# SiLU written with tanh, and half of the attention rows divided on ScalarE: an attention block with two feed-forward layers on one core

## The chip, the core and the metric

The kernel runs on one core of one Trainium2 chip. A core has TensorE (PE, with the weight loads PEld beside the matmuls), VectorE (DVE), ScalarE (ACT), GpSimd (POOL), and SyncE (SP), which issues the transfers. The metric is the device time of one execution in microseconds; lower is better.

## The reference, cut to what matters

Attention over 4 batches of 8 heads, 512 local and 32 global positions of 64 values, is followed by two feed-forward layers on 2176 tokens of 512 values. The first layer, which the change touches, is a gated SiLU with 1536 inner features; the second has 2048 inner features and a leaky ReLU with a slope per feature.

```python
def sm(s):
    s = s - np.max(s, axis=-1, keepdims=True)
    e = np.exp(s)
    return e / (np.sum(e, axis=-1, keepdims=True) + 1e-09)
...
def _moe_ref(x, w_gate, w_val, w_out):
    g = x @ w_gate
    silu = g * (1.0 / (1.0 + np.exp(-g)))
    val = x @ w_val
    return (silu * val @ w_out).astype(np.float32)
```

## The kernel before

The feed-forward products are made as three matmul passes over pairs of tiles: every operand is split into an upper part in a short format and the remainder, so each block of 128 features needs 12 matmuls (`mm12`, line 519). Weights arrive in a packed form and are converted on chip: two ScalarE passes (lines 454 and 455), three VectorE passes (456, 457, 460), a copy for the upper part (472 on ScalarE or 470 on VectorE) and a subtraction for the remainder (435, VectorE).

**Attention units.** A local unit is one pair of heads and one half (256 rows) of the positions; a batch has eight local units and two global ones. `s` makes the scores (line 171), takes the row maxima on VectorE (184) and the exponentials with their row sums on ScalarE (197). `n` makes the reciprocals of the sums (204, 205) and divides the four 128x256 pieces of the unit (207, VectorE). `t` transposes the result, for batches 0 and 1 on TensorE (229) with a ScalarE copy out of PSUM (154), and for batches 2 and 3 (`split`) by a DMA after a rounding to half precision (221, 222). `pv` makes the product with the values (250 or 241) and writes it into the token tile: for batch 0 straight into the operand `xa` of the first layer (264, 265), for the others to `yp` or `y3` (258).

**Stages.** The first units of batch 0 run ahead of everything else. Then `visit1` runs the first layer for one batch (or a part of its columns) and one half of the inner features (`GA` or `GB`), and `pump` puts the steps of the attention units between its pieces, so that batch 1 to 3 attention runs beside the first layer of batches 0 to 2. Each step of a unit is put into the queue in the order `s`, `t` of the unit before, `n`, `pv` of the one before that. The first layer of batch 3 has no attention beside it. The second layer (`visit2`) comes last.

**Inside visit1.** For a group of up to 512 columns: 12 or 24 matmuls into the PSUM bank `g`; `Silu` on ScalarE from that bank to the SBUF tile `sg` (576); the same number of matmuls into the bank `v`; their product on VectorE to `t` (585); the upper part `h` on ScalarE (589) and the remainder on VectorE (593, queued at the next `pump`). The matmuls of `down` (559) of a group run one or two groups later. There is one bank `g`, one bank `v`, one `sg` and one `t`. Work goes to the engines in order of priority and readiness as the framework plans it; each engine then runs its queue in that fixed order.

In the profile a load of ScalarE's function table (ACT_TABLE_LOAD) stands before the first exponential after a SiLU and before the first SiLU after an exponential. The copies and the Relus have none.

Of the kernel before, what the change touches and what calls it, by code (L numbers as in the profile page):

```python
# [17 lines left out]
ACTF = mybir.ActivationFunctionType  # L18
ALU = mybir.AluOpType
# [23 lines left out]
def kernel(  # L43
# [11 lines left out]
    nc = tc.nc  # L55
    HEAT, ND, NR, LAG = (P[i] for i in ("HEAT", "ND", "NR", "LAG"))

    def pr(name):
        off = P["pr_" + name]
        return tc.high_priority(off) if off else nullcontext()  # L60
# [3 lines left out]
    def frac(name):  # L64
        a = mix.get(name, 0.0) + P[name]
        mix[name] = a - int(a + 1e-9)
        return int(a + 1e-9) > 0
# [30 lines left out]
    def bank(tag):  # L98
        return ps.tile([128, 512], F32, tag=tag, name="ps_" + tag)
# [11 lines left out]
    def heat(n):  # L111
        t = bank("g")
        for _ in range(n):
            nc.tensor.matmul(out=t[:, 0:128], lhsT=zero, rhs=zero, start=True, stop=True)
# [44 lines left out]
    class Local(Unit):  # L159
# [42 lines left out]
        def n(self):  # L202
            rc = attp.tile([128, 4], F32, tag="rc", name="rc")
            nc.vector.tensor_scalar(out=rc, in0=self.sm, scalar1=1e-9, scalar2=None, op0=ALU.add)
            nc.vector.reciprocal(out=rc, in_=rc)
            for j in range(4):
                nc.vector.tensor_scalar(
                    out=self.e[:, j], in0=self.e[:, j], scalar1=rc[:, j:j + 1],
                    scalar2=PSC if self.split else None, op0=ALU.mult,
                    op1=ALU.mult if self.split else ALU.bypass,  # L210
                )
            if self.split and self.half == 0:
                self.pair.split_v()
# [137 lines left out]
    def later(n, f):  # L351
        due.setdefault(st["k"] + n, []).append(f)
# [141 lines left out]
    def weight(key):  # L494
        while key not in wt:
            if not wloaded and not wsplit and not wlo:
                wload()
            wpump()
        return wt[key]
# [6 lines left out]
    def passes(a, b):  # L506
        return ((a[0], b[0]), (a[0], b[1]), (a[1], b[0]))
# [5 lines left out]
    def mm12(o, w, c0, c1):  # L513
        i = 0
        for k in range(4):
            wk = [w[:, p, 128 * k:128 * k + 128] for p in range(2)]
            xk = [xa[:, p, k, c0:c1] for p in range(2)]
            for a, x in passes(wk, xk):
                nc.tensor.matmul(out=o, lhsT=a, rhs=x, start=(i == 0), stop=(i == 11))  # L519
                i += 1  # L520

    def ypieces(b, c0, c1):
        res = []
        for hf in range(2):
            a, z = max(c0, 256 * hf), min(c1, 256 * hf + 256)
            if a < z:
                res.append((lambda m, hf=hf, a=a, z=z: yh(b, hf)[:, m, a - 256 * hf:z - 256 * hf], a - c0, z - a))
        if c1 > S:
            res.append((lambda m: yg[:, m], S - c0, 128))
        return res  # L530
# [4 lines left out]
    def visit1(b, c0, c1, fs, last, pump, after_f=None, boundary=None, third=None):  # L535
        n = c1 - c0
        half = n == 256
        acc = [bank(f"acc{m}") for m in range(2 if half else 4)]
        if half:
            acc = [acc[m // 2][:, 256 * (m % 2):256 * (m % 2) + 256] for m in range(4)]  # L540
        hs = {}

        per = max(1, 512 // n)
        groups = [fs[i:i + per] for i in range(0, len(fs), per)]
        nn = n * per
        lag = 2 if third else 1

        def down(i):
            h = hs.pop(i)
            for q, f in enumerate(groups[i]):  # L550
                w = weight((1, f, "o"))
                opens = None
                for m in range(4):
                    wm = [w[:, p, 128 * m:128 * m + 128] for p in range(2)]
                    second = half and m % 2 == 1
                    for j, (a, x) in enumerate(passes(wm, [h[:, p, n * q:n * q + n] for p in range(2)])):
                        first = f == fs[0] and j == 0
                        with tc.issue_after(opens.ins) if first and second else nullcontext():
                            mm = nc.tensor.matmul(  # L559
                                out=acc[m][:, 0:n], lhsT=a, rhs=x,  # L560
                                start=(first and not second),
                                stop=(f == fs[-1] and j == 2 and (second or not half)),
                            )
                        if first:
                            opens = mm
                if after_f:
                    after_f(f, "o")

        for i, gf in enumerate(groups):
            pump()  # L570
            g = bank("g")
            for q, f in enumerate(gf):
                mm12(g[:, n * q:n * q + n], weight((1, f, "g")), c0, c1)
            sg = work.tile([128, 512], F32, tag="sg", name="sg")
            with pr("h"):
                nc.scalar.activation(out=sg[:, 0:nn], in_=g[:, 0:nn], func=ACTF.Silu)  # L576
            pump()
            v = bank("v")
            for q, f in enumerate(gf):
                mm12(v[:, n * q:n * q + n], weight((1, f, "v")), c0, c1)  # L580
                if after_f:
                    after_f(f, "gv")
            t = work.tile([128, 512], F32, tag="t", name="t")
            with pr("h"):
                nc.vector.tensor_tensor(out=t[:, 0:nn], in0=v[:, 0:nn], in1=sg[:, 0:nn], op=ALU.mult)  # L585
            h = third() if third and i % 3 == 2 else hp.tile([128, 2, 512], F32R, tag="h", name="h")
            hs[i] = h
            with pr("h"):
                nc.scalar.activation(out=h[:, 0, 0:nn], in_=t[:, 0:nn], func=ACTF.Copy)
            zh = "0" if st["k"] < mark[1] else "1" if st["k"] < mark[2] else "2" if st["k"] < mark[4] else "3"  # L590
            eng = nc.gpsimd if frac("hq" + zh) else nc.vector
            soon.append(
                lambda h=h, t=t, eng=eng: eng.tensor_tensor(
                    out=h[:, 1, 0:nn], in0=t[:, 0:nn], in1=h[:, 0, 0:nn], op=ALU.subtract
                )
            )
            pump()
            if i >= lag:
                down(i - lag)
        if boundary:  # L600
            boundary()
        for i in range(max(0, len(groups) - lag), len(groups)):
            down(i)
        with pr("acc"):
            for m in range(4):
                if (c0, c1) == (0, S):
                    dst = yp[b][:, :, m]
                    src = acc[m].rearrange("p (a c) -> p a c", a=2)
                    if last:
                        nc.vector.tensor_tensor(out=dst, in0=src, in1=dst, op=ALU.add)  # L610
                    else:
                        nc.scalar.activation(out=dst, in_=src, func=ACTF.Copy)
                    continue
                for dst, o, z in ypieces(b, c0, c1):
                    if last:
                        nc.vector.tensor_tensor(out=dst(m), in0=acc[m][:, o:o + z], in1=dst(m), op=ALU.add)
                    else:
                        nc.scalar.activation(out=dst(m), in_=acc[m][:, o:o + z], func=ACTF.Copy)
# [74 lines left out]
    if True:  # L693
# [47 lines left out]
        def reload(group, first):  # L741
# [9 lines left out]
            return after  # L751

        visit1(0, 0, 256, GA, False, pumper(P["ns0"], mark[1] + P["e0"], P["wr0"], P["g0"]), third=early)
        p = pumper(P["ns1"], mark[2] + P["e1"], P["wr1"], P["g1"])
        assert st["k"] >= mark[1] + LAG
        visit1(0, 256, 512, GA, False, p, after_f=reload(GB, GA), third=early)
        att_tags["list"] = ["a0", "a1"]
        visit1(0, 0, 512, GB, True, p, boundary=lambda: xprep(1), third=early)
        p = pumper(P["ns2"], mark[3] + P["e2"], P["wr2"], P["g2"])
        visit1(1, 0, 512, GB, False, p, after_f=reload(GA, GB), third=early)  # L760
# [122 lines left out]
```

## Time and profile before

| | |
|---|---|
| median of 3 runs (lowest to highest) | 967.0 us (966.22 to 967.29) |
| the profiled execution: its time | 967.48 us |
| its span, first to last instruction | 965.6 us |
| TensorE (PE) busy | 954.6 us (99%) |
| VectorE (DVE) busy | 540.8 us (56%) |
| ScalarE (ACT) busy | 478.0 us (49%) |
| mean granted TensorE clock | 0.991 |
| chain that ended last | PE 89%, ACT 5%, DMA 2%, DVE 2%, issue 1%, SPq 1% |

The span and what lies around it (967.48 - 965.6 = 1.9 us) make the execution's time. Matmuls overlap and their ends are modelled, so a busy PE isn't PE at its best pace; the pace is read from the length of pieces of the chain of waits. The busy shares of VectorE and ScalarE are averages over stages that differ much: both are far busier in the first 200 us than afterwards.

### The profile page before, as it was taken

What the parts mean: (1) busy time and instruction counts of PE and PEld (TensorE: products, weight loads), DVE (VectorE), ACT (ScalarE), POOL (GpSimd) and SP (SyncE); (2) the same over time, 40 slices, a digit from 0 to 9 for tenths busy, and PEclk for the clock granted to TensorE, in tenths of its full rate; (3) what the DMA queues carried; (4) which work ended last, traced back from release to release, by engine and by line L of the source; (5) the groups of instructions that cost most, each with busy time, mean ns of one, the idle gap of its engine ahead of it and who ended that gap; (6) DMA issues with size and microseconds to landing.
All of it is one profiled execution on the core that took longest, in us unless ns stands there. A gap on an engine that the chain in (4) does not pass through costs nothing.

```text
span 965.6 us, 14379 instructions
## 1 busy us (share of the span) xinstructions
PE 954.6 (99%) x5716; PEld 794.6 (82%) x5716; DVE 540.8 (56%) x1148; ACT 478.0 (49%) x892; POOL 0.7 (0%) x6
## 2 busy tenths in 40 slices
PE   8999999999999999999999999999999999999998
PEld 5678976777777777788999998888888888899897
DVE  6889799855454654518711399534433534444453
ACT  6789999855565666725422265223222322322332
POOL 0000000000000000000000000000000000000000
PEclk9799999999999999999999999999999999999999
DMA  8878775646643265702555052001000100010000
GB/s 278 307 272 330 304 281 219 226 114 205 181 141 73 61 174 167 182 4 88 175 199 193 1 175 87 1 1 44 1 1 0 44 1 1 1 44 1 20 14 23
DMA packets 56867, 111.83 MB, mean 116 GB/s; under 512 B 36448, under 2 KB 40544, under 8 KB 47456
## 3 DMA queue, kind: packets, MB, share of 16 engines
q1 hardware_dynamic: 56800, 110.91, 34.6%
q8 instruction: 45, 0.74, 0.3%
q14 instruction: 22, 0.18, 0.1%
HBM read 79.18 MB, written 23.33 MB: 106 GB/s over the span
## 4 chain that ended last, share of the span: by engine, by line
PE 89%; ACT 5%; DMA 2%; DVE 2%; issue 1%; SPq 1%; ACTq 0%
PE ps_acc L653 19%; PE ps_g L519 18%; PE ps_v L519 18%; PE ps_acc L559 13%; PE ps_a L519 10%; PE ps_a L171 3%; PE ps_a L241 2%; DMA dbl<-in_w_dram 2%; ACT e L197 1%; PE ps_a L325 1%; PE ps_a L250 1%; ACT raw L454 1%; PE ps_a L282 1%; PE ps_acc L250 1%; ACT dbl L455 1%
## 5 line engine op out<-in xcount | busy, mean ns | idle before, releaser
L519 PE MATMUL ps_g<-xa,w 128*128 128x512 f32 (+2 forms) x1032 | 207.7, 349 | 0.3 <-ACT sg L576 0.3
L519 PE MATMUL ps_v<-xa,w 128*128 128x512 f32 (+2 forms) x1032 | 205.7, 348 | 0.0
L519 PEld LDWEIGHTS ps_g<-xa,w 128*128 128x128 f32 x1032 | 168.5, 189 | 27.4 <-issue 6.0
L519 PEld LDWEIGHTS ps_v<-xa,w 128*128 128x128 f32 x1032 | 168.9, 189 | 25.8 <-issue 5.7
L653 PE MATMUL ps_acc<-w,h 128*128 128x512 f32 x561 | 138.0, 392 | 0.0
L653 PEld LDWEIGHTS ps_acc<-w,h 128*128 128x128 f32 x561 | 104.6, 188 | 22.0
L559 PE MATMUL ps_acc<-h,w 128*128 128x512 f32 (+2 forms) x600 | 119.2, 350 | 0.0
L559 PEld LDWEIGHTS ps_acc<-h,w 128*128 128x128 f32 x600 | 97.8, 189 | 15.4 <-issue 3.0
L519 PE MATMUL ps_a<-xa,w 128*128 128x512 f32 (+2 forms) x480 | 100.8, 359 | 0.0
L519 PEld LDWEIGHTS ps_a<-xa,w 128*128 128x128 f32 x480 | 83.5, 188 | 13.4
L585 DVE TENSOR_TENSOR t<-ps_v,sg 128x512 f32<-128x512 f32 (+1 forms) x54 | 35.7, 661 | 104.1 <-PE ps_v L519 89.4
L671 ACT ACTIVATE h<-g 128x512 fp32r<-128x512 f32 (+2 forms) x55 | 31.3, 568 | 76.1 <-DVE g L670 76.1
L197 ACT ACTIVATE e<-e,mx 128x256 f32<-128x256 f32 x128 | 63.8, 502 | 10.3 <-DVE mx L184 9.6
L653 PE MATMUL ps_acc<-w,hx 128*128 128x512 f32 x255 | 63.1, 394 | 0.0
L184 DVE CUSTOM_DVE_ANT_0 e<-ps_a,lm 128x256 f32<-128x256 f32 x102 | 37.9, 421 | 43.3 <-PE ps_a L171 42.3
L667 DVE TENSOR_SCALAR g<-ps_a,alpha 128x512 f32<-128x512 f32 (+2 forms) x40 | 26.8, 671 | 61.0 <-ACT r L666 60.4
L653 PEld LDWEIGHTS ps_acc<-w,hx 128*128 128x128 f32 x255 | 47.5, 188 | 10.4
L666 ACT ACTIVATE r<-ps_a 128x512 f32<-128x512 f32 (+2 forms) x40 | 21.3, 533 | 62.5 <-PE ps_a L519 62.1
L672 DVE TENSOR_TENSOR h<-g,h 128x512 fp32r<-128x512 f32 (+2 forms) x55 | 33.7, 612 | 33.1 <-ACT h L671 33.1
L576 ACT ACTIVATE sg<-ps_g 128x512 f32<-128x512 f32 (+1 forms) x54 | 31.0, 575 | 40.5 <-PE ps_g L519 40.1
L670 DVE TENSOR_TENSOR g<-g,r 128x512 f32<-128x512 f32 (+2 forms) x80 | 49.0, 612 | 2.5
L576 ACT ACT_TABLE_LOAD x30 | 38.5, 1283 | 19.9 <-PE ps_g L519 19.4
(133 smaller groups left out, 1089.8 us busy)
## 6 DMA issues: line engine op xcount, KB each, us to landing
dbl<-in_w_dram SPq DMA_DIRECT2D x28, 1024.0 KB, 5.4
qk<-in_qk_dram SPq DMA_DIRECT2D x12, 592.0 KB, 6.4
yp<-in_w_dram SPq DMA_DIRECT2D x6, 1024.0 KB, 8.4
out_dram<-o SPq DMA_DIRECT2D x16, 256.0 KB, 2.1
v<-in_v_dram SPq DMA_DIRECT2D x12, 320.0 KB, 4.1
w<-w1s0g SPq DMA_DIRECT2D x2, 1024.0 KB, 4.8
w<-w1s1g SPq DMA_DIRECT2D x2, 1024.0 KB, 4.8
w<-w1s2g SPq DMA_DIRECT2D x2, 1024.0 KB, 5.1
```

Source lines behind the costliest of these rows:

```text
L171: nc.tensor.matmul(out=s[h][:, 256 * i:256 * i + 256], lhsT=x[rows, WIN + 128 * t:WIN + 128 * t + 128], rhs=x[rows, 128 * t:128 * t + 256] ...
L184: nc.vector.tensor_tensor_reduce(out=self.e[:, j], in0=s[h][:, 256 * i:256 * i + 256], in1=lm[:, 2 * self.half + i], scale=-0.125, scalar= ...
L197: nc.scalar.activation(out=self.e[:, j], in_=self.e[:, j], func=ACTF.Exp, scale=-1.0, bias=mx[:, j:j + 1], accum_out=self.sm[:, j:j + 1],)
L519: nc.tensor.matmul(out=o, lhsT=a, rhs=x, start=(i == 0), stop=(i == 11))
L559: mm = nc.tensor.matmul(out=acc[m][:, 0:n], lhsT=a, rhs=x, start=(first and not second), stop=(f == fs[-1] and j == 2 and (second or not h ...
L576: nc.scalar.activation(out=sg[:, 0:nn], in_=g[:, 0:nn], func=ACTF.Silu)
L585: nc.vector.tensor_tensor(out=t[:, 0:nn], in0=v[:, 0:nn], in1=sg[:, 0:nn], op=ALU.mult)
L653: nc.tensor.matmul(out=acc[t], lhsT=a, rhs=x, start=(i == 0 and j == 0), stop=(i == NF2 - 1 and j == 2))
L667: nc.vector.tensor_scalar(out=g[:, 0:n], in0=u[:, 0:n], scalar1=0.0, scalar2=alpha[:, f:f + 1], op0=ALU.min, op1=ALU.mult)
L670: nc.vector.tensor_tensor(out=g[:, 0:n], in0=g[:, 0:n], in1=r[:, 0:n], op=ALU.add)
L671: nc.scalar.activation(out=h[:, 0, 0:n], in_=g[:, 0:n], func=ACTF.Copy)
L672: nc.vector.tensor_tensor(out=h[:, 1, 0:n], in0=g[:, 0:n], in1=h[:, 0, 0:n], op=ALU.subtract)
```

## The change

SiLU is rewritten: g times sigmoid(g) is g times (1 + tanh(g/2)) / 2. ScalarE makes the tanh with a scale of 0.5, and VectorE makes (tanh + 1) times g, read from the bank `g`, and then half of that times v. The four divisions of a local unit of batches 0 and 1 (8 units each, 64 divisions) move from VectorE to ScalarE, as a copy with a scale per row. Batches 2 and 3 keep theirs, and so do the global units.

```diff
             for j in range(4):
+                if not self.split:
+                    nc.scalar.activation(
+                        out=self.e[:, j], in_=self.e[:, j], func=ACTF.Copy, scale=rc[:, j:j + 1]
+                    )
+                    continue
                 nc.vector.tensor_scalar(
                     out=self.e[:, j], in0=self.e[:, j], scalar1=rc[:, j:j + 1],
...
             with pr("h"):
-                nc.scalar.activation(out=sg[:, 0:nn], in_=g[:, 0:nn], func=ACTF.Silu)
+                nc.scalar.activation(out=sg[:, 0:nn], in_=g[:, 0:nn], func=ACTF.Tanh, scale=0.5)
             pump()
...
             with pr("h"):
-                nc.vector.tensor_tensor(out=t[:, 0:nn], in0=v[:, 0:nn], in1=sg[:, 0:nn], op=ALU.mult)
+                nc.vector.scalar_tensor_tensor(
+                    out=sg[:, 0:nn], in0=sg[:, 0:nn], scalar=1.0, in1=g[:, 0:nn], op0=ALU.add, op1=ALU.mult
+                )
+                nc.vector.scalar_tensor_tensor(
+                    out=t[:, 0:nn], in0=sg[:, 0:nn], scalar=0.5, in1=v[:, 0:nn], op0=ALU.mult, op1=ALU.mult
+                )
```

## Rows read from the trace of the kernel before

**Rows 1.** By stretch: busy us (instructions) of PE, PEld, DVE, ACT, POOL; clock; DMA.

```profile
0.00:48.00 48.00, 42.48 (x222) 28.30 (x223) 35.48 (x112) 34.88 (x79) 0.70 (x6) 0.82 0.83 292
48.00:97.00 49.00, 49.00 (x424) 40.93 (x422) 43.39 (x113) 45.98 (x92) 0.00 (x0) 1.00 0.83 303
97.00:193.00 96.00, 95.37 (x689) 75.32 (x686) 82.28 (x185) 88.68 (x155) 0.00 (x0) 1.00 0.70 257
193.00:410.00 217.00, 217.00 (x1469) 167.78 (x1466) 112.66 (x329) 134.98 (x266) 0.00 (x0) 1.00 0.52 144
...
560.00:600.00 40.00, 39.85 (x205) 36.20 (x204) 38.77 (x55) 24.45 (x31) 0.00 (x0) 1.00 0.40 140
```

**Rows 2.** Chain of waits: start us, length us, what, and how many instructions.

```profile
80.13 1.06 PE ps_a L171 x4
...
162.67 0.44 PE ps_a L229 x4
...
187.89 1.06 PE ps_a L171 x8
188.95 2.94 PE ps_g L519 x12
...
205.58 2.72 PE ps_g L519 x12
```

**Rows 3.** Matmul groups of 97 to 193 us, 18 rows: the first and last.

```profile
L519 PE MATMUL ps_g<-xa,w 128*128 128x512 f32 x72 | 19.1, 405 | 0.3 <-ACT sg L576 0.3
...
L171 PE MATMUL ps_acc<-qk 64*128 64x256 f32 x4 | 1.1, 402 | 0.0
```

**Rows 4.** Table loads of the whole span: line, count, busy us, mean ns, idle before.

```profile
L576 ACT ACT_TABLE_LOAD x30 | 38.5, 1283 | 19.9 <-PE ps_g L519 19.4
...
L197 ACT ACT_TABLE_LOAD x24 | 30.8, 1283 | 11.4 <-DVE mx L184 10.3 <-PEq L874 0.7
...
L300 ACT ACT_TABLE_LOAD x6 | 7.7, 1283 | 0.1
```

**Rows 5.** Table loads of two stretches: first 48 to 97 us, then 97 to 193 us.

```profile
L576 ACT ACT_TABLE_LOAD x3 | 3.8, 1283 | 0.1
L197 ACT ACT_TABLE_LOAD x3 | 3.8, 1283 | 0.1
...
L576 ACT ACT_TABLE_LOAD x9 | 11.5, 1283 | 0.6 <-PE ps_g L519 0.4
L197 ACT ACT_TABLE_LOAD x6 | 7.7, 1283 | 0.1
L300 ACT ACT_TABLE_LOAD x2 | 2.6, 1283 | 0.0
```

**Rows 6.** Single operations of the whole span, by form.

```profile
L197 ACT ACTIVATE e<-e,mx 128x256 f32<-128x256 f32 x128 | 63.8, 502 | 10.3 <-DVE mx L184 9.6
...
L207 DVE TENSOR_SCALAR e<-e,rc 128x256 f32<-128x256 f32 x128 | 37.1, 350 | 0.9
L457 DVE SCALAR_TENSOR_TENSOR dbl<-dbl 128x1024 int32<-128x1024 int32 x28 | 34.3, 1225 | 6.7 <-ACT dbl L455 6.6
...
L585 DVE TENSOR_TENSOR t<-ps_v,sg 128x512 f32<-128x512 f32 x42 | 29.0, 690 | 76.2 <-PE ps_v L519 65.0 <-issue 3.1 <-ACT e L197 3.1
...
L258 ACT ACTIVATE yp<-ps_a 128x256 f32<-128x256 f32 x16 | 6.1, 384 | 6.0 <-PE ps_a L241 4.5 <-PE ps_a L250 1.4
```

**Rows 7.** Line 207 by stretch: DVE busy us (instructions), clock, DMA share.

```profile
0.00:48.00 48.00, 7.08 (x24) 0.82 0.83 292
48.00:97.00 49.00, 5.01 (x18) 1.00 0.83 303
```

**Rows 8.** Line 585 by stretch, with the same columns.

```profile
97.00:193.00 96.00, 5.51 (x8) 1.00 0.70 257
```

**Rows 9.** Timeline of ScalarE: start us, length us, instruction, idle before it.

```profile
41.70 0.37 ACT L264 ACTIVATE xa<-ps_a 128x256 fp32r<-128x256 f32 x1
...
579.51 1.16 ACT L454 ACTIVATE raw<-dbl 128x1024 f32<-128x1024 f32 x1 [1.77 <-DMA dbl<-in_w_dram]
```

## The prediction, made blind

> **What bounds the kernel now.** I read the busy time by stretches first. Up to 193 us three engines are all nearly full; from there to 410 us ScalarE is busy for 134.98 of 217 us and VectorE for 112.66, under a TensorE that never stops, so work taken from either buys nothing there by itself [rows 1]. The change can act in three places: the start (0 to 48 us), the stretch in which both helpers are full (48 to 193 us), and 560 to 600 us, where VectorE is busy for 38.77 of 40 us with the weights of the second layer.
>
> Then I asked how much time TensorE loses where it is called busy. The chain of waits gives the pace: 12 matmuls of 512 columns take 2.72 us at best, a full set of scores (eight records) 1.06 us, four transposes 0.44 us [rows 2]. From 97 to 193 us, 18 groups of matmuls stand in the trace [rows 3]: 168 of 512 columns and 192 of 256 in the feed-forward layer (38.1 and 23.0 us at such paces), the rest attention (28.0 us, each form at the length of its shortest piece in the chain). That is 89.1 us of 96, so 6.9 us are lost. Part of that never comes back: the first 12 matmuls after an attention piece take 2.94 instead of 2.72 us [rows 2], and some 14 such changes in the stretch make 3.1 us. About 3.8 us can be won there, however free ScalarE becomes. From 48 to 97 us the same count gives 7.0 us lost, of which up to 4.2 come from the four units whose scores run in two pieces of four, each as long as the eight together [rows 2]. That is a matter of when their two banks come free.
>
> **Part 1: the table loads.** There are 30 + 24 + 6 = 60 loads of 1283 ns [rows 4]. If tanh and the exponential share a table, one is left: 59 x 1.283 = 75.7 us less of ScalarE. By stretch: none before 48 us, 6 from 48 to 97 us (7.7 us), 17 from 97 to 193 us (21.8 us) [rows 5], nearly all of the rest before 410 us, where ScalarE isn't the limit. No row shows whether the two functions share one; this is a rival below.
>
> One rule would make this worth more. From 97 to 193 us ScalarE is busy for 88.68 of 96 us with 17 loads in it [rows 1, 5]; 7.3 us are idle, 0.43 us a load, so a load costs hardly more than its own 1.28 us. The Trainium skill (ScalarE: Activation LUTs, What ACT_TABLE_LOAD costs) adds a drain of about 1380 ns to each switch, 2.66 us in all; by it the 59 would be 157 us. The trace disagrees: 17 drains would be 23.5 us, and there is no room for them. I keep 1.283.
>
> **Part 2: the divisions.** Of 64, 24 lie before 48 us, 18 in the next stretch [rows 7], 22 after. VectorE gives back 0.350 us each (22.4 us). On ScalarE no row has this form. Bounds by the nearest rows: 0.384 us, the same size with a constant scale, and 0.502 us, with an operand per row (line 197) [rows 6]. I take 0.45, nearer to the one with the operand: 28.8 us (24.6 to 32.1). So a division costs ScalarE more than it gives VectorE. The Trainium skill speaks against the move (ScalarE: Activation LUTs, Rules for kernel authors): multiplications belong on VectorE. Its estimate for an activation with an operand per row, 280 ns + 0.833 ns an element, is 0.493 us here and would make 31.6 us of the 64; row 0.502 of a like operation agrees.
>
> **Part 3: the sum and the products.** One product of 0.690 us at 512 columns becomes two operations. No row has the new form on these types; a scalar_tensor_tensor of 1024 elements takes 1225 ns [rows 6], half of which is 0.61, and the old product with one operand in PSUM takes 0.690. I take 0.69 for each, so one of 0.69 is added (0.61 to 0.69). It falls 3 times (one a group, from the code) between 48 and 97 us, 8 times from 97 to 193 us [rows 8]; all 54 make about 36 us.
>
> The bank `g` was released by ScalarE after Silu; now VectorE does it after the sum. Queued behind that on VectorE are `t`, the remainders and the weights; who waits is the next group's first matmul. In between TensorE has the 12 matmuls into `v`, 2.72 us, against tanh (0.6, as Silu is) and the sum (0.69): 1.4 us in hand. I cost it at nothing; if VectorE is later than that at a place with no other matmul in between, it costs the difference (rival below).
>
> **The sum by stretch,** against the profiled execution's own 967.5 us (span 965.6 and 1.9 around it), which is 0.5 above the median of 967.0.
>
> *0 to 48 us.* ScalarE gets 24 x 0.45 = 10.8 us on top of 34.88, VectorE loses 8.4 of 35.48 [rows 1]. The first layer waits for the tokens of the first four units; the last of their copies starts at 41.70 us [rows 9] at the end of a nearly unbroken run of ScalarE work. The divisions of three units queued ahead of it (12 x 0.45 = 5.4 us) move into that run, and 12 x 0.35 = 4.2 us leave VectorE's, part of the same path. Net 1.2 us if all of the relief counts, 5.4 if none, 0 if they fit in ScalarE's idle time. I take +2.0 (0 to +5.4).
>
> *48 to 97 us.* ScalarE: 18 x 0.45 - 7.7 = +0.4 us of 45.98; VectorE: 3 x 0.69 - 18 x 0.35 = -4.2 of 43.39. ScalarE stays as full as it was. I take -1.0 (-4.2 to 0).
>
> *97 to 193 us.* ScalarE: 22 x 0.45 - 21.8 = -11.9 of 88.68; VectorE: 8 x 0.69 - 22 x 0.35 = -2.2 of 82.28. ScalarE is clearly relieved, but TensorE can give back only 3.8. I take -2.5 (-3.8 to 0).
>
> *193 to 560 us.* 0: TensorE covers both changes; without that cover, VectorE's added sums would be some 27 us.
>
> *560 to 600 us.* VectorE is full and gets a sum more a group. The last `down` of the first layer waits for a remainder whose upper part stands behind a conversion on ScalarE that begins at 579.51 us, held by a transfer [rows 9], which waits in turn for VectorE to free its buffer. Four sums ahead of that are 4 x 0.69 = 2.8 us at most. I take +1.5 (0 to +2.8).
>
> Together 2.0 - 1.0 - 2.5 + 1.5 = 0.0: 967.5 for that execution, 967.0 against the median.
>
> **The rivals.** About 0.2% (1.9 us) is what a measurement of this kernel can tell from no change.
>
> *Forecast, within 0.2%: 0.36.* Own range 965.1 to 968.9.
>
> *Faster: 0.34.* The divisions leave a crowded VectorE queue and run at once, so the start costs nothing, and the relief of both engines is collected: 0 - 4.2 - 3.8 + 0 = -8.0 at most, 959; half of it, 963, is likelier. For it: both engines are full up to 193 us. Against it: the pool is 8 us, most of it a matter of bank order.
>
> *Slower, the start: 0.22.* The place is ScalarE's queue ahead of the copy of line 264. If the divisions add more there than later stretches return (3.5 us), the kernel is slower: +5.4 + 0 - 1.0 + 2.8 = +7.2, 974; the middle is 971. It decides once that copy starts after about 46 us. For it: ScalarE runs nearly unbroken there. Against it: VectorE's queue is on the same path and shrinks.
>
> *Slower, bank `g`: 0.05.* At the start of each part of the first layer up to 193 us, where no `down` stands between two groups, a sum 1 us late five times makes +5: 972. Against it: `t`, at the same place in the queue, is not waited for by TensorE now.
>
> *Slower, the loads stay: 0.03.* If tanh and the exponential don't share a table, nothing is saved and the divisions come on top: 45.98 + 8.1 is 5 us over the 49 of its stretch, 88.68 + 9.9 is 2.6 over 96, and +2 at the start: +10, 977. The Trainium skill (ScalarE: Activation LUTs, Table sets: the hidden batching unit) lists tanh with exp in one set; no run here shows it yet.
>
> The chances follow: faster 0.34, same 0.36, slower 0.30. The range is 961 to 972: it holds the likely middles of both sides and leaves out the full sum of either, about 0.2.
>
> **What would show it.** One table load in all. Divisions on ScalarE between 0.384 and 0.502 us. ScalarE's busy share from 97 to 193 us down to about 0.8, near 0.94 before 97 us, VectorE about unchanged there. The fourth copy of line 264 some 2 us later than 41.70; the second layer beginning at about the same time as before. What would make the prediction wrong: more than 4 us won or lost before 97 us, since the order of the queues there is replanned and the scores could run whole or in pieces in other units; or a TensorE wait for line 587's sum.

## The result, and the profile after

The changed kernel takes 976.35 us (median of 4 runs, 974.9 to 976.89) against 967.04 of the kernel before (966.22 to 967.29): a ratio of 1.0094, 95% interval 1.0081 to 1.0106. It is 9.3 us slower and lies 4.4 us above the predicted range. The profiled execution took 976.71 us, with a span of 974.9.

**Where the time went.** Windows of the changed kernel, in the columns and stretches of [rows 1]:

```profile
0.00:48.00 48.00, 32.28 (x149) 19.85 (x151) 25.36 (x76) 35.53 (x83) 0.70 (x6) 0.73 0.79 271
48.00:97.00 49.00, 49.00 (x416) 38.68 (x413) 38.27 (x94) 46.44 (x106) 0.00 (x0) 0.99 0.78 285
97.00:193.00 96.00, 95.82 (x682) 78.41 (x681) 83.07 (x169) 78.53 (x166) 0.00 (x0) 1.00 0.73 271
193.00:410.00 217.00, 216.88 (x1471) 167.65 (x1470) 122.77 (x343) 88.23 (x227) 0.00 (x0) 1.00 0.52 140
...
560.00:600.00 40.00, 40.00 (x223) 38.63 (x221) 38.28 (x57) 22.87 (x31) 0.00 (x0) 1.00 0.38 132
```

Against [rows 1] only the first line has collapsed: 149 TensorE instructions before 48 us instead of 222, at a granted clock of 0.73 instead of 0.82, and VectorE down by 10.1 us. ScalarE's share there has hardly risen, 35.53 against 34.88, although 20 divisions were added: other work of it that ran before 48 us now runs later. From 193 to 410 us it is relieved of 46.7 us, and the kernel gains nothing by that.

What ScalarE did ahead of the fourth copy into `xa`, which stands at 41.70 us before and at 56.26 after (the columns of [rows 1]; first the kernel before, then the changed one):

```profile
0.00:41.70 41.70, 36.24 (x183) 23.66 (x183) 30.66 (x99) 30.91 (x73) 0.70 (x6) 0.80 0.88 301
0.00:56.26 56.26, 40.54 (x205) 25.42 (x206) 31.15 (x88) 43.08 (x101) 0.70 (x6) 0.76 0.74 256
```

ScalarE's work ahead of that copy (its busy time, fourth in the row) has grown by 12.2 us: 24 divisions, 10.1 us by themselves, and its part of one more weight tile (lines 459, 460 and 477), some of which overlaps.

When TensorE begins the n-th of the 12-matmul feed-forward products' matmuls (us, read from the trace by line 519 before and 524 after) tells the same:

```
matmul             1st   24th   96th   192nd   384th   1401st   1632nd   end of span
before            38.7   48.2   70.8    99.8   171.0    532.3    597.5      965.6
after             46.6   58.2   81.0   110.1   180.5    542.1    606.8      974.9
later by           7.9   10.0   10.2    10.3     9.5      9.8      9.3        9.3
```

All of it is lost before the 24th matmul. Timeline of ScalarE in the changed kernel (start, length, instruction, idle time before it and what ended it):

```profile
0.73 1.28 ACT L197 ACT_TABLE_LOAD   x1 [0.73 <-PEq L884]
...
9.50 1.70 ACT L208 ACTIVATE e<-e,rc 128x256 f32<-128x256 f32 x4 [0.66 <-DVE rc L205]
...
14.55 1.12 ACT L459 ACTIVATE raw<-dbl 128x1024 f32<-128x1024 f32 x1 [1.87 <-DMA dbl<-in_w_dram]
15.56 1.12 ACT L460 ACTIVATE dbl<-dbl 128x1024 int32<-128x1024 uint32 x1
16.59 1.07 ACT L154 ACTIVATE pt<-ps_acc 128x512 f32<-128x512 f32 x2
17.54 1.70 ACT L208 ACTIVATE e<-e,rc 128x256 f32<-128x256 f32 x4
...
24.24 1.06 ACT L154 ACTIVATE pt<-ps_a 128x512 f32<-128x512 f32 x2
...
26.40 1.71 ACT L208 ACTIVATE e<-e,rc 128x256 f32<-128x256 f32 x4
...
33.64 0.38 ACT L269 ACTIVATE xa<-ps_v 128x256 fp32r<-128x256 f32 x1
37.63 1.06 ACT L477 ACTIVATE w<-raw 128x1024 fp32r<-128x1024 f32 x1 [3.61 <-DVE raw L465]
38.60 1.70 ACT L208 ACTIVATE e<-e,rc 128x256 f32<-128x256 f32 x4
...
45.15 1.70 ACT L208 ACTIVATE e<-e,rc 128x256 f32<-128x256 f32 x4
46.75 0.37 ACT L269 ACTIVATE xa<-ps_acc 128x256 fp32r<-128x256 f32 x1
...
54.66 1.70 ACT L208 ACTIVATE e<-e,rc 128x256 f32<-128x256 f32 x4
56.26 0.37 ACT L269 ACTIVATE xa<-ps_a 128x256 fp32r<-128x256 f32 x1
```

Its timeline for TensorE and for VectorE:

```profile
17.22 1.11 PE L255 MATMUL ps_acc<-pt,v 128*64 128x256 f32 x2 [5.52 <-ACT pt L154]
...
24.87 0.80 PE L255 MATMUL ps_v<-pt,v 128*64 128x256 f32 x2 [1.77 <-ACT pt L154]
...
30.85 1.22 PE L171 MATMUL ps_a<-qk 64*128 64x256 f32 x2
32.00 1.11 PE L234 MATMUL ps_g<-ident,e 128*128 128x128 f32 x4
...
33.26 0.42 DVE L184 CUSTOM_DVE_ANT_0 e<-ps_a,lm 128x256 f32<-128x256 f32 x1 [5.49 <-PE ps_g L234]
...
39.15 1.54 PE L234 MATMUL ps_acc<-ident,e 128*128 128x128 f32 x6 [3.80 <-ACT e L208]
40.62 0.69 PE L255 MATMUL ps_acc<-pt,v 128*64 128x128 f32 x2
...
46.61 1.01 PE L524 MATMUL ps_g<-xa,w 128*128 128x256 f32 x3
```

And two lines of the kernel before, from its timelines of ScalarE and TensorE:

```profile
11.66 1.09 ACT L154 ACTIVATE pt<-ps_acc 128x512 f32<-128x512 f32 x2 [0.53 <-PE ps_acc L229]
...
38.69 0.51 PE L519 MATMUL ps_g<-xa,w 128*128 128x256 f32 x2
```

Read them together. Before, the copy of the first transposes (line 154) runs at 11.66 us, ahead of the first weight conversion. After, the conversion (459, 460) stands ahead of it and waits for its DMA until 14.55: the copy runs at 16.59, and TensorE stops for 5.52 us. From there to 25.2 us ScalarE runs without a gap: the second unit's division at 17.54, a weight copy, two conversion passes and four exponentials stand ahead of that unit's copy at 24.24 (1.77 us more for TensorE). Then a wait goes round three engines. VectorE, with the fifth unit's row maxima at the head of its queue, is idle for 5.49 us until TensorE has made that unit's last scores (30.85) and the transposes behind them (32.00), whose end the trace names as what released it; ScalarE, with a weight copy (477) at the head, is idle for 3.61 us until VectorE has converted those weights; and the fourth unit's division, behind that copy, starts at 38.60 (its reciprocals on VectorE, behind the same conversion, had ended at 37.89). TensorE is idle for 3.80 us, and the last two matmuls of the third unit's product (40.62) stand behind the fourth unit's transposes. What follows is ScalarE's queue, which runs without a gap while each of the two products waits in it: that product ends at 41.3 us, and its copy, the third into `xa`, starts only at 46.75, behind four exponentials, a conversion and the fifth unit's division (45.15) among others. The fourth product ends at 50.1 us, and its copy, which stood at 41.70 us [rows 9], follows at 56.26, behind the sixth unit's division (54.66).

The price of the single operations, groups by line and form (count, busy us, mean ns, idle before):

```profile
L593 DVE SCALAR_TENSOR_TENSOR t<-sg,ps_v 128x512 f32<-128x512 f32 x42 | 28.7, 684 | 22.1 <-PE ps_v L524 21.9
L590 DVE SCALAR_TENSOR_TENSOR sg<-sg,ps_g 128x512 f32<-128x512 f32 x42 | 28.7, 683 | 53.0 <-ACT sg L581 53.0
L208 ACT ACTIVATE e<-e,rc 128x256 f32<-128x256 f32 x64 | 27.3, 509 | 1.2 <-DVE rc L205 1.2
```

### The profile page after: what moved, and what is told of

Read it like the earlier page. It is cut to its first block, busy times and chain, and to the rows that moved or that the text cites. A ratio compares the mean times of both kernels' runs of the same rounds, so it can differ in the third digit from the quotient of the medians.

```text
span 974.9 us, 14330 instructions
## 1 busy us (share of the span) xinstructions
PE 954.1 (98%) x5716; PEld 793.9 (81%) x5716; DVE 556.0 (57%) x1138; ACT 426.6 (44%) x897; POOL 0.7 (0%) x6
## 4 chain that ended last, share of the span: by engine, by line
PE 91%; ACT 4%; DVE 3%; DMA 1%; SPq 1%; issue 1%; DVEq 0%
PE ps_acc L663 19%; PE ps_g L524 19%; PE ps_v L524 18%; PE ps_acc L564 13%; PE ps_a L524 10%; PE ps_a L171 3%; PE ps_a L246 2%; PE ps_a L330 1%; ACT e L197 1%; PE ps_a L255 1%; DMA dbl<-in_w_dram 1%; ACT e L208 1%; PE ps_a L287 1%; PE ps_a L234 1%; PE ps_acc L234 1%
## 5 line engine op out<-in xcount | busy, mean ns | idle before, releaser
L590 DVE SCALAR_TENSOR_TENSOR sg<-sg,ps_g 128x512 f32<-128x512 f32 (+1 forms) x54 | 35.3, 654 | 67.4 <-ACT sg L581 67.3
L599 ACT ACTIVATE h<-t 128x512 fp32r<-128x512 f32 (+1 forms) x42 | 25.7, 611 | 62.6 <-DVE t L593 62.5
L593 DVE SCALAR_TENSOR_TENSOR t<-sg,ps_v 128x512 f32<-128x512 f32 (+1 forms) x54 | 35.3, 655 | 29.1 <-PE ps_v L524 28.9
```

The source lines that it names most:

```text
L590: nc.vector.scalar_tensor_tensor(out=sg[:, 0:nn], in0=sg[:, 0:nn], scalar=1.0, in1=g[:, 0:nn], op0=ALU.add, op1=ALU.mult)
L593: nc.vector.scalar_tensor_tensor(out=t[:, 0:nn], in0=sg[:, 0:nn], scalar=0.5, in1=v[:, 0:nn], op0=ALU.mult, op1=ALU.mult)
```

## The experiments

**Theory.** The loss is made in the first 48 us: on ScalarE each division of batch 0 stands in an in-order queue behind work that has nothing to do with it, on the path to the first layer's tokens. **Rivals:** (1) the tanh part, by the sum on VectorE and the bank `g`; (2) the missing table loads, by another order of the queues; (3) the order of the first copy alone; (4) the number of added divisions, so much for each. The kernel before, run again beside them, took 967.42 us (29 runs) beside the first four, 967.29 (29) beside the next four, 967.27 (18) beside the last two; differences in us are those of the medians. What the milestones say for each:

```
                          median     ratio (95% interval)    1st   96th   192nd   384th   4th copy  ahead
before                                                      38.7   70.8    99.8   171.0     41.7     30.9
after                     976.35   1.0094 (1.0081-1.0106)   46.6   81.0   110.1   180.5     56.3     43.1
tanh part alone           968.24   0.9997 (0.9986-1.0008)   38.6   69.3   102.8   172.1     41.8     30.9
divisions alone           984.89   1.0172 (1.0155-1.0189)   42.5   78.5   111.8   181.6     52.4     43.1
4 units back on VectorE   968.13   1.0017 (1.0001-1.0034)   39.2   73.4   101.9   172.8     48.2     37.2
table loads alone         965.74   0.9985 (0.9976-0.9993)   38.7   70.1    99.6   169.6     41.3     31.0
first copies first        975.09   1.0068 (1.0045-1.0090)   37.8   73.9   101.7   173.9     49.5     43.1
2 units back on VectorE   968.48   1.0009 (0.9998-1.0019)   39.3   73.6   101.4   171.9     47.7     39.9
divisions of batch 1      969.33   1.0012 (0.9998-1.0025)   39.1   69.4    99.9   170.5     41.8     30.9
before, conversion first  970.05   1.0028 (1.0018-1.0038)   43.6   75.2   104.2   175.5     45.6     30.8
only 2 units on ScalarE   968.12   1.0009 (0.9999-1.0020)   41.7   72.2   101.7   171.7     44.4     33.0
weight copy on VectorE    969.53   1.0024 (1.0014-1.0034)   42.7   76.5   104.6   175.6     47.6     35.8
```

(Median of the timed runs; the other columns are from each profiled execution, which can be far from the median: start of the n-th feed-forward matmul, start of the fourth copy into `xa`, and us of ScalarE work ahead of that copy.)

**Tanh part alone** (the two hunks on SiLU, divisions as before).

> Only the tanh part; all 64 divisions stay on VectorE. Theory A (the whole loss is the divisions of the first units, queued on ScalarE ahead of the copies out of PSUM): the first layer's first matmul is back at 38.7 us (46.6 with the change) and the time is that of before less what the saved table loads give, 963 to 967 us. Rival B (the loss is VectorE's added sums and the later release of bank g): 970 us or more, and the first matmul of the layer still at 38.7.

Measured: no difference; the median is 1.2 us above A's range. Its start is that of the kernel before, so rival 1 doesn't make the loss. Nor does the tanh part gain by its median: four of the twelve runs took 964.02 to 965.32 us, the others 967.91 to 968.93, and the profiled one (968.36) is of the slower group. Windows of two stretches in it:

```profile
72.00:84.00 12.00, 10.73 (x104) 9.03 (x104) 12.00 (x35) 11.03 (x25) 0.00 (x0) 1.00 0.82 319
84.00:92.00 8.00, 8.00 (x45) 6.59 (x43) 5.38 (x12) 5.52 (x10) 0.00 (x0) 0.57 0.63 262
```

A line of its timeline of TensorE:

```profile
83.05 1.36 PE L325 MATMUL ps_acc<-ptg,v 128*64 128x32 f32 x40 [1.14 <-DVE mx L184]
```

With the divisions still on it VectorE is busy for all of 72 to 84 us, TensorE waits 1.14 us for its row maxima, and then the granted clock is 0.57, near the lower of its two levels (1.2 GHz), up to 92 us. At the 96th matmul this kernel is 1.5 us ahead of the kernel before, at the 192nd 3.0 behind.

**Divisions alone** (the first hunk, with Silu).

> Only the divisions of batches 0 and 1 move to ScalarE; SiLU and its product stay as before, so the 60 table loads stay too. A: the first copies and the first matmul of the layer as late as with the full change (46.6 us), time 975 to 982 us, since the loads that stay cost a little more beside the divisions. B: 967 to 970 us.

Measured: 17.5 us slower, nearly twice the whole change and beyond A's range, though its first matmul comes at 42.5 us and not at 46.6 (the profiled execution is the fastest of its four, 980.61). Its fourth copy starts at 52.4 us, and it goes on losing afterwards: 7.7 us late at the 96th matmul, 10.6 at the 384th, 13.0 at the end of the span. So the division is what costs, and the tanh part, worth nothing by itself, is worth 8.5 us when ScalarE carries the divisions too.

**Four units back on VectorE** (the four that run ahead of everything; the rest of the change as it is).

```diff
-                if not self.split:
+                if not self.split and (self.pair.b or self.half):
```

> The full change, but the four units of the first half of batch 0 (16 of the 64 divisions) are divided on VectorE. A: the start is as before (fourth copy of line 264 near 42 us instead of 56), 963 to 968 us. A variant of A, that all units ahead of the first layer matter: in between, 969 to 973. B: 975 or more.

Measured: 0.7 us slower by the medians, 1.6 by the ratio (966.49 to 975.66); 16 of the 64 divisions back on VectorE take back nearly all of the 9.3 us. The fourth copy comes at 48.2 us all the same, not near the expected 42. Two of the twelve runs took 974.0 and 975.66 us.

**Table loads alone** (Tanh in place of Silu, nothing else; it leaves out the scale, the sum with 1 and the products with g and a half).

```diff
-                nc.scalar.activation(out=sg[:, 0:nn], in_=g[:, 0:nn], func=ACTF.Silu)
+                nc.scalar.activation(out=sg[:, 0:nn], in_=g[:, 0:nn], func=ACTF.Tanh)
```

> The kernel of before with tanh in place of SiLU (this leaves out the multiplication by g and the halves, so the output is another function): the table loads go, VectorE's work and the divisions are as before. It gives what the loads alone are worth. By the count of the prediction 2 to 4 us (963 to 965 us); if TensorE's covered waits are worth more than counted, 955 to 961; if the queues' plan decides, anything within 3 us of 967.

Measured: 1.7 us faster, the only run clearly under the kernel before. Its window from 97 to 193 us:

```profile
97.00:193.00 96.00, 96.00 (x693) 77.06 (x692) 81.72 (x184) 69.46 (x142) 0.00 (x0) 1.00 0.70 260
```

ScalarE is down by 19.2 us against [rows 1], and that stretch gains 1.2 us (99.6 to 169.6 against 99.8 to 171.0). Rival 2 is out: the start is as before.

**First copies first** (the full change; the copies of line 154 of the first units get a higher priority, which puts them ahead of the first conversion again).

```diff
-            evac(self.pt[:, h], t, "cp0" if st["k"] < mark[0] + LAG else "cp1")
+            with tc.high_priority(60) if st["k"] < mark[0] + LAG else nullcontext():
+                evac(self.pt[:, h], t, "cp0" if st["k"] < mark[0] + LAG else "cp1")
```

> The full change, with all its work, but the copies of the first units' transposes out of PSUM (line 154) get priority, so that those of the first unit stand ahead of the first weight conversion in ScalarE's queue, as in the kernel before, and not behind it. If the place in the queue makes the loss (A1): the first copy at about 11.5 us instead of 16.6, the first matmul of the layer near 40 to 42 us, 967 to 971 us. If the added ScalarE work itself makes it (A2): the first copy early, but the fourth copy of line 264 still near 55 us and 974 or more.

Measured: 975.09, between 970.46 and 977.65; the profiled execution is the fastest of them. Windows of ScalarE's fullest stretches:

```profile
12.00:24.00 12.00, 6.13 (x30) 3.64 (x31) 8.02 (x18) 11.95 (x27) 0.00 (x0) 0.82 0.91 338
24.00:36.00 12.00, 9.83 (x57) 5.92 (x53) 10.59 (x30) 11.90 (x29) 0.00 (x0) 0.89 0.89 298
36.00:48.00 12.00, 9.30 (x69) 5.63 (x68) 8.01 (x21) 11.95 (x30) 0.00 (x0) 1.00 0.82 308
```

A line of its timeline of TensorE:

```profile
20.52 1.97 PE L234 MATMUL ps_a<-ident,e 128*128 128x128 f32 x8 [5.10 <-ACT e L208]
```

The 5.52 us wait for the first copy is gone, and TensorE waits 5.10 us for the second unit's division instead. ScalarE is now busy for 35.80 of 36 us, with the same 43.1 us of work ahead of the fourth copy as in the full change; that copy comes at 49.5 us, 6.8 earlier than there and 7.8 later than in the kernel before. So with the first copies in their old place the length of the queue still costs, and their order alone isn't what the change lacks. The expectation's two cases split: this execution's time is in the first one's range, the median in the second's, and none of the slower runs was profiled.

**Before, conversion first** (the kernel before; only the first unit's two copies are queued behind the first conversion).

```diff
-            evac(self.pt[:, h], t, "cp0" if st["k"] < mark[0] + LAG else "cp1")
+            with tc.issue_after(conv_ops[0]) if self is units[0] and conv_ops else nullcontext():
+                evac(self.pt[:, h], t, "cp0" if st["k"] < mark[0] + LAG else "cp1")
...
```

(The lines that keep each conversion's second pass in `conv_ops` are left out.)

> The kernel of before in all its work, with one order changed: the two copies of the first unit's transposes stand behind the first weight conversion in ScalarE's queue, which waits for a transfer until 14.5 us. A1: this alone costs 3 to 6 us (970 to 973 us), the first matmul of the layer 3 us or more later than 38.7. A2: within 1 us of before.

Measured: 2.8 us slower with no operation added. Its line of TensorE's timeline:

```profile
16.83 1.11 PE L251 MATMUL ps_acc<-pt,v 128*64 128x256 f32 x2 [2.56 <-ACT pt L154]
```

Its 30.8 us of ScalarE work ahead of the fourth copy are those of the kernel before, and the copy comes at 45.6 us instead of 41.7. Rival 3 can be part of the loss and isn't the whole of it: two copies put behind one conversion make 2.8 us here, against 9.3.

**Two units back on VectorE** (8 of the 64 divisions).

```diff
-                if not self.split:
+                if not self.split and (self.pair.b or self.half or self.pair.p > 1):
```

> The full change, but the first two units (8 of 64 divisions) are divided on VectorE; units three and four of the first half stay on ScalarE. A1 (what costs is the first units' place ahead of and behind the first conversion): 967 to 971 us. A2 (each unit's division on ScalarE costs the start about the same, some 2.3 us a unit): 971 to 973.

Measured: 1.2 us slower, with an interval that holds no change. Eight divisions back on VectorE return 8 of the 9.3 us. Yet TensorE still has one wait nearly as long as the 5.52 us of the full change, now for the third unit's copy:

```profile
29.25 2.45 PE L255 MATMUL ps_acc<-pt,v 128*64 128x256 f32 x12 [5.26 <-ACT pt L154]
```

So no single wait of that length is the loss.

**Divisions of batch 1 only** (none before 48 us on ScalarE).

```diff
-                if not self.split:
+                if not self.split and self.pair.b:
```

> The tanh part and the divisions of batch 1 alone on ScalarE (32), those of batch 0 on VectorE. The start is as before; from 97 to 193 us VectorE is lighter than with the tanh part alone. If VectorE's load in that stretch held the gain of the loads back: 962 to 965 us. If the loads are worth only the 1.7 us seen alone: 965 to 968.

Measured: 2.0 us slower by the medians, with an interval that holds no change, and above both expected ranges; the start is that of the kernel before. No version here that computes the reference's function has a median below that of the kernel before.

**Only two units on ScalarE** (the same eight divisions, now alone).

```diff
-                if not self.split:
+                if not self.split and self.pair.b == 0 and self.half == 0 and self.pair.p < 2:
```

> The tanh part, and of the 64 divisions only the eight of the first two units on ScalarE; the other 56 stay on VectorE. Theory (these eight alone carry the loss, since ScalarE is what the first layer's tokens wait for there): 974 to 977, first matmul of line 524 after 43 us. Rival (the loss grows with the number of divisions before 48 us, 24 of them): a third of 9, so 969 to 972.

Measured: 0.9 us slower, with an interval that holds no change, and below what either expects. The theory in the form in which these eight alone carry the loss falls, and so does rival 4: 8 on ScalarE cost 0.9 us, the other 56 cost 1.2, all 64 cost 9.3. ScalarE's timeline shows why they aren't enough:

```profile
15.42 1.08 ACT L154 ACTIVATE pt<-ps_acc 128x512 f32<-128x512 f32 x2
...
33.29 0.37 ACT L269 ACTIVATE xa<-ps_v 128x256 fp32r<-128x256 f32 x1
33.55 1.06 ACT L477 ACTIVATE w<-raw 128x1024 fp32r<-128x1024 f32 x1
...
35.42 0.36 ACT L269 ACTIVATE xa<-ps_acc 128x256 fp32r<-128x256 f32 x1
...
44.38 0.37 ACT L269 ACTIVATE xa<-ps_a 128x256 fp32r<-128x256 f32 x1
```

A line of its timeline of TensorE:

```profile
33.35 1.98 PE L255 MATMUL ps_acc<-pt,v 128*64 128x256 f32 x12
```

The first copy of line 154 is late (15.42 us, against 11.66 in the kernel before), and the second copy into `xa` starts at 33.29, as in the full change (33.64). But the third follows 2.1 us later instead of 13.1: the third unit's product runs whole, not as ten matmuls and two behind another unit's transposes, and the weight copy of line 477 starts without a wait. With the later divisions on VectorE the start catches up.

**Weight copy on VectorE** (the full change; the upper copy of the split weights, line 477, runs on VectorE in the first stage).

```diff
-    lo0=0.0, lo1=0.0, lo2=0.0, lo3=0.0, hi0=0.0, hi1=0.25, hi2=0.25, hi3=0.5,
+    lo0=0.0, lo1=0.0, lo2=0.0, lo3=0.0, hi0=1.0, hi1=0.25, hi2=0.25, hi3=0.5,
```

> The full change, with the rounding copy of the split weights (line 477) put on VectorE for the whole of the first stage: about 1 us a tile less for ScalarE, four tiles before 48 us, and about as much more for VectorE. Theory 'ScalarE's length': the start gets shorter by some 3 to 4 us, 971 to 974. Rival 'VectorE is as full, or the chain between the engines sets it': 975 to 979.

Measured: 969.53; with every division still on ScalarE, 7.0 of the 9.3 us come back, more than the theory's 2 to 5, and no wait of TensorE for a division is listed up to 56 us, though 8.3 us of waits for copies of line 154 are. Taking other work out of the queue does nearly as much as taking away the divisions. About 1 us a tile leaves ScalarE by it, so it is shorter as well as differently ordered, and the run doesn't tell the two apart.

## Why the prediction was wrong

The forecast was "within 0.2%"; the rival *Slower, the start* happened, beyond its full sum. By its own steps:

- **0 to 48 us, +2.0 (0 to +5.4): the step that failed.** Measured +10.0 at the 24th matmul. The place was right (ScalarE's queue ahead of the copy of line 264), and so was the sign; the size was not, for three reasons. First, the count: 12 divisions, of three units, were put ahead of the fourth copy. In the order of the steps, in which a unit's product comes after the divisions of two later units, six units' divisions stand there, and the trace has all 24 (9.50, 17.54, 26.40, 38.60, 45.15 and 54.66 us) and one more weight tile: 12.2 us of work and not 5.4. Second, VectorE's relief was subtracted, but VectorE only stood idle for longer (25.36 us busy before 48 us, against 35.48); and the relief was taken as 0.350 us each, while [rows 7] has 7.08 us for 24. Third, waits that the queue passes on were priced at nothing: one unit's copies behind one conversion cost 2.8 us with no length added, and where the fourth unit's division stood behind a weight copy that waited, TensorE was idle for 3.80 us and the third copy into `xa` came at 46.75 us, against 35.42 where that division was on VectorE. The prediction's own sign of being wrong, more than 4 us lost before 97 us because the queues are replanned, came true with 10; it had no term for it.
- **48 to 97 us, -1.0.** From the 24th to the 192nd matmul the lag went from 10.0 to 10.3 us: nothing won. ScalarE's share before 97 us is 0.85 and not the predicted 0.94, since its idle time before 48 us did not fill up (12.5 us, against 13.1 in the kernel before).
- **97 to 193 us, -2.5.** The lag shrank by 0.8 us to the 384th matmul; the loads alone gave 1.2. TensorE has no listed wait left there, and 19.2 us less of ScalarE (loads alone) won no more than that; what holds the rest of the 6.9 us that it loses, no run shows.
- **193 to 560 us, 0.** +0.3 (9.5 to 9.8): right. The 46.7 us that ScalarE gains there buy nothing.
- **560 to 600 us, +1.5.** -0.5 (9.8 to 9.3): the added sums on the full VectorE were covered.
- **Single costs.** Sums and products were taken as 0.69 us: 0.683 and 0.684. A division takes 0.509 us by itself, just over the upper bound of 0.502, and 0.427 of ScalarE's time on average (27.3 / 64), as those in a row overlap. On VectorE it took 0.290 of the engine's time (37.1 / 128 [rows 6]); the difference is 3.3 us for the 24 divisions, so most of the loss isn't that. There is one table load, so tanh and the exponential share a set. The Trainium skill lists them so (ScalarE: Activation LUTs, Table sets: the hidden batching unit), and the trace agrees. The Trainium skill's rule that multiplications belong on VectorE (ScalarE: Activation LUTs, Rules for kernel authors) agrees with 0.290 against 0.427.
- **The rivals.** *Slower, bank `g`* is out: no TensorE wait for the sum of line 590 is listed. *The loads stay* is out. *Faster* assumed the divisions would run at once: the second unit's began 4.1 us after its reciprocals (13.47 to 17.54 us), and the one of 38.60 us 0.7 us after its own, which were late too. Its other half, the relief, was worth 1.7 us (loads alone). The rival's point of decision, the fourth copy after about 46 us, was passed by 10 us. As a rule it was too simple: the runs with that copy at 47.6 to 48.2 us cost 0.7 to 2.3 us, and one with it at 45.6 cost 2.8.

**The cause, as far as shown.** Shown: the loss needs divisions of batch 0 on ScalarE (divisions alone, divisions of batch 1, and two or four units back); it isn't in proportion to their number, since 8 cost 0.9 us, the other 56 cost 1.2 and all 64 cost 9.3; and taking any of three things off ScalarE's queue in the first stage (8 divisions, 16 divisions, the weight copies) brings 7 to 8.6 us back. The last column of the table puts these together: the three kernels with 43.1 us of ScalarE work ahead of the fourth copy lose 7.8 to 17.5 us, the others, with 39.9 or less, lose 2.8 at most. Shown in part: order adds to that (conversion first, 2.8 us; and the same 43.1 us of work put that copy at 49.5, 52.4 or 56.3 us). Shown by the trace alone: the wait that goes round VectorE, ScalarE and TensorE between 27.8 and 39.15 us.

Why up to 39.9 us are nearly free is read from the milestones and not tested: the stretch behind has slack. Eight of the twelve kernels reach the 96th matmul between 69.3 and 73.9 us, and all eight reach the 192nd between 99.6 and 102.8, in no order; those that come to the 96th at 75 us or later stay late. What sets that floor was not tried; VectorE, full from 72 to 84 us in the tanh kernel, is a candidate. How the 9.3 us split between length, order and the clock stays open, because each edit replans all the queues.

## What to carry to other kernels

An operation moved to another engine joins an in-order queue: count everything that the queue's order puts ahead of the result that the next stage needs (here six units' work for the fourth unit's copy), and add what that waits for, a DMA or another engine. Relief is worth only what the engine that sets the end was losing to it: 59 table loads, 75.7 us of ScalarE, were worth 1.7 us. Move work that feeds the first stage last, and try the parts apart: here 8 of the divisions were nearly free, the other 56 too, and all 64 were not.

## What the runs showed of the hardware

A pause of TensorE can be followed by a lower granted clock and then costs more than its length. In the tanh kernel 1.14 us of waiting at 82 us is followed by 8 us at 0.57, and between the 96th and the 192nd matmul that kernel falls from 1.5 us ahead of the kernel before to 3.0 behind. Not every pause does so: *divisions of batch 1* has two shorter waits at the same place, 0.51 and 0.47 us, and keeps its clock:

```profile
72.00:84.00 12.00, 10.87 (x103) 8.74 (x102) 11.82 (x31) 12.00 (x30) 0.00 (x0) 1.00 0.84 317
84.00:92.00 8.00, 8.00 (x71) 7.16 (x68) 7.10 (x20) 8.00 (x21) 0.00 (x0) 1.00 0.89 357
```

What decides between the two, no run shows. In the changed kernel TensorE is busy for 23.75 of the 36 us from 12 to 48, and the granted clock is 0.72, 0.57 and 0.62 in the three stretches of 12 us; in the kernel before it is busy for 32.40 of them, at 0.84, 0.50 and 0.95.

Over the first 60 us the granted clock (full speed is 2.4 GHz, the lower level 1.2) is 0.77 in the changed kernel and 0.86 before. That is an estimated 5 us of full-speed TensorE time (0.09 x 60), the most of the 9.3 us that the lower clock can hold. It can't be the whole loss: the profiled executions of *divisions alone* and *first copies first* had 0.91 and 0.94 there and reached the 96th matmul 7.7 and 3.1 us late. Of the runs of *first copies first* the longer ones had the lower mean clock: 970.46 us at 0.996, 971.75 and 974.52 at 0.993, 975.65 to 977.65 at 0.988 and 0.985. Which of the two is cause there, no trace shows.
